# Writing the instruction order out by hand to the end of the first chunk's recurrence

## The chip, the cores and the metric

The kernel runs on one core of one Trainium2 chip. The metric is the device time of one execution in microseconds, the median of several runs. Five engines take part, each with its own queue that runs in order: PE (TensorE, matmuls), DVE (VectorE), ACT (ScalarE), POOL (GpSimd, only at the start), and SP (SyncE), which here only issues DMAs. PEld in a view is PE loading weights beside its matmuls.

## The reference

Three stages follow each other: a recurrence with gates over 768 time steps (4 batches, 8 heads of 40 channels), then two gated feed-forward layers on its 3072 x 320 output.

```python
# recurrence, per batch and head, for each t
m_new = np.maximum(f_gate[t] + m, i_gate[t])
f_stab, i_stab = np.exp(f_gate[t] + m - m_new), np.exp(i_gate[t] - m_new)
C = f_stab * C + i_stab * outer(v[t], k[t])
n = f_stab * n + i_stab * k[t]
y[t] = sigmoid(o_gate[t]) * (C @ q[t]) / np.maximum(np.abs(n @ q[t]), 1.0)
# first layer, 320 -> 1536 -> 320
x = (sigmoid(x @ w_gate) * (x @ w_val)) @ w_out
# second layer, 320 -> 2048 -> 320
h = x @ w_in
out = (h * np.clip(h + 3, 0, 6) / 6) @ w_out
```

All of it is fp32.

## The kernel before

The sequence is cut into six chunks of 128 steps. A chunk of the four batches gives 512 tokens, and these go through both layers with the tokens along the free axis. The recurrence of chunk c and batch b is three pieces: `att0` (scores q.k in `scores`, the decay factors by a scan in `decays`, values scaled by the input gate, `values_end`, `weigh`), `att1` (`outputs`, `denominators`, `gated`, `state`) and `att2` (three PE transposes, then a split of the result into a high part xh on ACT and a low part xl on DVE). The decay scan of L385 needs rows of the gate factors spread over all partitions. For chunk 0 and batches 0 and 1 PE does that (`spread`); for all others a DMA reads them back from a DRAM buffer, `fz_dram` (`dec_load`, L219), which a store on SP fills first. `later_chunks` does this store for chunks 1 to 5 (L291) after a small DVE write (L289, L290), then the scan of L292, two groups of five small transposes (L278) with copies to iT and gT, and five products (L301) for one matmul (L305).

Every fp32 matmul is done as three matmuls in a reduced format, with each operand split into a high and a low part. So every weight tile has to be converted. Its 64-bit source comes by DMA into one of three `raw` buffers (`fetch`, L88); ACT makes `u` (L98), DVE the fp32 bits (L115, L118), ACT the high part (L139, L141, or L161 for an output weight) and DVE the low part (L147, L151, or L167, L170). The conversions stand in the list `jobs`: two input weights, one output weight, and so on.

The first layer is a row of steps. A step is `m1_h` (16 matmuls, L547 to L554, into two PSUM banks), on ACT a sigmoid (L573), on DVE the product g (L574), on ACT its high part gh (L560), on DVE its low part gl (L561), and later `m1_out` (eight matmuls, L589 and L599, into three banks of the pool `acc`). In chunk 0 the first four weight tiles are used in halves: first all four on batches 0 and 1 (256 columns), then all four on batches 2 and 3. The other steps have 512 columns. In what follows blocks 1 to 4 are the four steps on the first half, and step 4 is the next one.

The pools of PSUM banks hold three `mm`, three `acc` and two `att`. A tile that finds no free bank waits until a reader of an older one is done.

Two things set the order. Inside `tc.manual_schedule()` (L656 to L719) every engine gets its instructions in the order in which the code is written. Behind it a scheduler orders them by its own costs, and it may also put instructions of later code between the written ones where the engine has nothing ready by these costs. `tc.issue_after(i)` holds instructions back until i is placed. Before the change the written order ends with the transposes of batches 0 and 1 (L709), two conversions and their state; pieces of batches 2 and 3 of chunk 0 are handed out among the first steps by the loop at L746, together with `work`, which converts one or two weight tiles a step.

Of the kernel before, what the change touches and what calls it, by code (L numbers as in the profile page):

```python
# [18 lines left out]
B, H, S, D = 4, 8, 768, 40  # L19
# [7 lines left out]
T = B * L  # L27
F1 = 1536 // P
# [4 lines left out]
def mlstm_then_two_gated_ffn(  # L33
# [69 lines left out]
    def to_f32(r, u=None):  # L103

        lower = r.bitcast(I32).rearrange("p (n two) -> p two n", two=2)[:, 0, :]
        u = scaled(r) if u is None else u
        bits = gpool.tile([P, 640], I32, tag="bits", name="bits")
        nc.vector.tensor_scalar(  # L115
            out=bits, in0=u.bitcast(I32), scalar1=3, scalar2=None, op0=ALU.logical_shift_left
        )
        nc.vector.scalar_tensor_tensor(  # L118
            out=bits, in0=lower, scalar=29, in1=bits,
            op0=ALU.logical_shift_right, op1=ALU.bitwise_or,  # L120
        )
        return bits.bitcast(F32)
# [11 lines left out]
    def hi_in(key, x):  # L134


        w = new_slot(key)
        xm = x[:, 0:512].rearrange("p (j n) -> p j n", j=2)
        nc.scalar.copy(out=w[:, :, 0:256], in_=xm)  # L139
        for j, a, b in halves_in:  # L140
            nc.scalar.copy(out=w[a, j, 256:384], in_=x[a, 512:640])  # L141
        return w

    def lo_in(w, x):
        wf = w.bitcast(F32)
        xm = x[:, 0:512].rearrange("p (j n) -> p j n", j=2)
        nc.vector.tensor_tensor(  # L147
            out=w[:, :, 384:640], in0=xm, in1=wf[:, :, 0:256], op=ALU.subtract
        )
        for j, a, b in halves_in:  # L150
            nc.vector.tensor_tensor(  # L151
                out=w[b, j, 256:384], in0=x[a, 512:640], in1=wf[a, j, 256:384], op=ALU.subtract
            )
# [4 lines left out]
    def hi_out1(key, x):  # L158

        w = new_slot(key)  # L160
        nc.scalar.copy(out=w[:, :, 0:320], in_=x.rearrange("p (j n) -> p j n", j=2))  # L161
        return w

    def lo_out1(w, x):
        wf = w.bitcast(F32)
        r = x.rearrange("p (j n) -> p j n", j=2)
        nc.vector.tensor_tensor(  # L167
            out=w[:, :, 320:384], in0=r[:, :, 256:320], in1=wf[:, :, 256:320], op=ALU.subtract
        )
        nc.vector.tensor_tensor(  # L170
            out=w[:, :, 384:640], in0=r[:, :, 0:256], in1=wf[:, :, 0:256], op=ALU.subtract
        )
# [45 lines left out]
    def dec_load(c, b):  # L218
        nc.sync.dma_start(  # L219
            out=at[c, b]["dec"].rearrange("p h l -> p (h l)"),  # L220
            in_=fz_dram[c, b * H : (b + 1) * H, :]
            .rearrange("h l -> (h l)")
            .rearrange("(o n) -> o n", o=1)
            .to_broadcast([P, H * L]),
        )
# [7 lines left out]
    def stabilise(a, b):  # L233


        m_old, m_new = m_sb[:, a:b], m_sb[:, a + 1 : b + 1]
        f, i = f_sb[:, a:b], i_sb[:, a:b]
        nc.vector.tensor_tensor_scan(
            out=m_new, data0=f, data1=i,
            initial=-1e30 if a == 0 else m_sb[:, a : a + 1], op0=ALU.add, op1=ALU.max,  # L240
        )
        yield
        nc.vector.tensor_tensor(out=f, in0=f, in1=m_old, op=ALU.add)
        yield
        nc.vector.tensor_tensor(out=f, in0=f, in1=m_new, op=ALU.subtract)
        yield
        nc.scalar.activation(out=fz_sb[:, a:b], in_=f, func=AF.Exp)
        yield
        nc.vector.tensor_tensor(out=i, in0=i, in1=m_new, op=ALU.subtract)
        yield  # L250
        last_exp.append(nc.scalar.activation(out=i, in_=i, func=AF.Exp).ins)
        yield
# [151 lines left out]
    def out_gate(c, b):  # L404
        o = at[c, b]["vko"][:, 2, :]
        nc.scalar.activation(out=o, in_=o, func=AF.Sigmoid)
# [118 lines left out]
    def att2(c, b, ps):  # L525
        yo = at.pop((c, b))["yo"]
        x_ps = ps()
        for k in range(3):
            nc.tensor.transpose(
                out=x_ps[:, k * P : (k + 1) * P], in_=yo[:, k * P : (k + 1) * P], identity=ident  # L530
            )
        x_v = x_ps[:, : 3 * P].rearrange("p (k t) -> p k t", k=3)
        xs = slice(b * L, (b + 1) * L)
        hi = nc.scalar.copy(out=XH[1, c][:, :, xs], in_=x_v)
        lo = nc.vector.tensor_tensor(
            out=XL[1, c][:, :, xs], in0=x_v, in1=XH[1, c].bitcast(F32)[:, :, xs], op=ALU.subtract
        )
        return hi.ins, lo.ins
# [87 lines left out]
    jobs = []  # L626
# [29 lines left out]
    with tc.manual_schedule():  # L656
        qk_load(0, 0)
        vko_load(0, 0)
        qk_load(0, 1)
        raws = [fetch(jobs[-1][0])]  # L660
        vko_load(0, 1)
        for _ in stabilise(0, L):
            pass
        nc.sync.dma_start(out=fz_dram[0], in_=fz[:, 0, :])
        raws += [fetch(jobs[-2][0]), fetch(jobs[-3][0])]
        for b in range(2, B):
            qk_load(0, b)
            vko_load(0, b)
            dec_load(0, b)
        later = stabilise(L, S)  # L670
        first, second = spread(0), spread(1)
        next(later)
        next(later)
        next(first)
        transpose_rows(i_c, iT, range(0, 1))
        decays(0, 0, 0)
        next(first)
        next(later)
        next(later)
        decays(0, 0, 1)  # L680
        scores(0, 0, any_ps)
        value_ones(0, 0)
        values(0, 0, False)
        u = scaled(raws[0])
        values_end(0, 0, False)
        next(later)
        next(later)
        for n in range(2):
            weigh(0, 0, n)
            next(second)  # L690
        x0 = to_f32(raws[0], u)
        scores(0, 1, any_ps)
        for n in range(2):
            decays(0, 1, n)
        value_ones(0, 1)
        values(0, 1, False)
        values_end(0, 1, False)
        for b in range(2):
            out_gate(0, b)
        w0 = hi_in(jobs.pop()[2], x0)  # L700
        outputs(0, 0, any_ps)
        for n in range(2):
            weigh(0, 1, n)
        outputs(0, 1, any_ps)
        gated(0, 0, denominators(0, 0), False)
        u = scaled(raws[1])
        lo_in(w0, x0)
        gated(0, 1, denominators(0, 1), False)
        for b in range(2):  # L709
            opened = att2(0, b, any_ps)  # L710
        x1 = to_f32(raws[1], u)
        w1_ = hi_in(jobs.pop()[2], x1)
        u = scaled(raws[2])
        lo_in(w1_, x1)
        x2_ = to_f32(raws[2], u)
        wo_ = hi_out1(jobs.pop()[2], x2_)
        lo_out1(wo_, x2_)
        for b in range(2):
            state(0, b)  # L719

    with tc.issue_after(opened[0]), tc.issue_after(opened[1]):
        later_chunks()
# [10 lines left out]
    steps = [step for c in range(NC) for step in tile_steps(c)]  # L733


    pieces = [(0, b, piece) for b in (2, 3) for piece in range(3)]
    for c in range(1, NC):
        for b in range(B):
            pieces += [(c, b, 0)] + [(c, b - 1, 2)] * (b > 0) + [(c, b, 1)]
# [2 lines left out]

    quota = [2, 2] + [1] * 4 + [0, 1] * 4 + [1] * (n_first - 14) + [1, 1, 0, 1, 0, 1]
    quota += [1] * (len(steps) - len(quota))
    before = []
    for i, (c, f, ts) in enumerate(steps):  # L746
        if i == halves[0] - 1:
            for b in range(2):
                att_load(1, b)
                dec_load(1, b)  # L750
        for _ in range(quota[i]):
            if pieces:
                cp, b, piece = pieces.pop(0)
                if cp > 0 and b == 0 and piece == 0:
                    x_tiles((1, cp))
                with ExitStack() as queued:
                    for ins in opened if cp == 0 else ():
                        queued.enter_context(tc.issue_after(ins))
                    (att0, att1, att2)[piece](cp, b, ps_att)
                nxt = divmod(cp * B + b + 2, B)  # L760
                if cp > 0 and piece == 2 and nxt[0] < NC:
                    att_load(*nxt)
                    dec_load(*nxt)
        gate = m1_h(c, f, ts)
        if before:
            m1_out(*before)
            if before[1] == F1 - 1:
                m1_end(before[0])
        before = (c, f, ts)
        if c == 0:  # L770
            work(1 if i < 2 * halves[0] else 2, n_w1)
        elif c < NC - 1:

            with tc.issue_after(gate):
                work(c > 1 and f % 2 == 0, n_conv)
        elif f == 0:
            work(F2, n_conv)
        else:
            work(f > 1, n_jobs)
        if c == NC - 1 and f == 6:  # L780
            x_split(0)
# [125 lines left out]
```

## Time and profile before

| | us |
|---|---|
| median of 3 runs | 875.86 (875.47 to 877.73) |
| the profiled execution | 874.0 |
| its span | 872.0 |
| PE busy / idle in the span | 844.7 / 27.3 |
| DVE busy | 516.2 |
| ACT busy | 347.5 |

Busy time is the sum over the whole span. The kernel has stages with different limits, so a share of 59% for DVE says nothing of a stretch of 50 us; the view by stretches does. The 27.3 us of PE idle are 872.0 less 844.7.

### The profile page before, as it was taken

How to read it: one execution, taken by the hardware profiler on the slowest of the kernel's cores; microseconds unless marked ns; L12 is line 12 of the kernel's file. 1: busy time of each engine (PE TensorE's matmuls, PEld its weight loads, DVE VectorE, ACT ScalarE, POOL GpSimd, SP SyncE). 2: the span in 40 equal slices, each digit the busy share in tenths (PEclk: the TensorE clock that was granted, in tenths of full speed). 3: DMA queues.
4: the chain of work that ended last, by engine and by line, in shares of the span. 5: the costliest groups of instructions: out<-in, count | busy, mean ns of one | idle time of the engine just before them, and what ended most of it. 6: DMA issues, size and time to landing. Idle time of an engine off the chain costs nothing.

```text
span 872.0 us, 17027 instructions
## 1 busy us (share of the span) xinstructions
PE 844.7 (97%) x7205; PEld 726.5 (83%) x7205; DVE 516.2 (59%) x930; ACT 347.5 (40%) x685; POOL 2.5 (0%) x8
## 2 busy tenths in 40 slices
PE   6599999999999999999999999999999999999998
PEld 6488678888788878878888888999999999999997
DVE  7899967776676777667545544344343353443433
ACT  3687634222333332342226445343343343433333
POOL 1000000000000000000000000000000000000000
PEclk9999999999999999999999999999999999999999
DMA  9645632232444355454203321001010010000000
GB/s 351 233 139 184 232 103 109 81 135 71 154 162 157 123 198 161 164 181 162 80 1 97 91 82 73 1 25 43 1 67 1 1 67 2 31 1 1 31 1 30
DMA packets 24923, 83.43 MB, mean 96 GB/s; under 512 B 2576, under 2 KB 5840, under 8 KB 24848
## 3 DMA queue, kind: packets, MB, share of 16 engines
q1 hardware_dynamic: 24800, 82.26, 27.7%
q8 instruction: 56, 0.92, 0.4%
q14 instruction: 19, 0.16, 0.1%
q10 hardware_dynamic: 48, 0.10, 0.0%
HBM read 68.35 MB, written 13.99 MB: 94 GB/s over the span
## 4 chain that ended last, share of the span: by engine, by line
PE 83%; DVE 4%; DMA 2%; issue 1%; ACT 0%; DVEq 0%
PE mm L551 11%; PE mm L553 11%; PE mm L552 11%; PE acc L589 10%; PE mm L547 6%; PE mm L554 6%; PE acc L813 5%; PE acc L812 5%; PE acc L811 5%; PE acc L599 3%; PE att L359 2%; DMA dec<-fz_dram 2%; PE att L813 2%; PE att L812 2%; PE att L811 2%; PE att L441 1%
## 5 line engine op out<-in xcount | busy, mean ns | idle before, releaser
L551 PE MATMUL mm<-xh,w 128*128 128x512 f32 (+1 forms) x520 | 195.8, 376 | 0.2 <-issue 0.2
L553 PE MATMUL mm<-xh,w 128*128 128x512 f32 (+1 forms) x520 | 194.8, 375 | 0.0
L552 PE MATMUL mm<-xl,w 128*128 128x512 f32 (+1 forms) x520 | 194.8, 375 | 0.0
L560 ACT CAST gh<-g 128x512 fp32r<-128x512 f32 (+1 forms) x178 | 106.1, 596 | 202.9 <-DVE g L574 111.5
L561 DVE TENSOR_TENSOR gl<-g,gh 128x512 fp32r<-128x512 f32 (+1 forms) x178 | 117.7, 661 | 112.9 <-ACT gh L560 112.3
L793 DVE SCALAR_TENSOR_TENSOR g<-g,mm 128x512 f32<-128x512 f32 x96 | 66.1, 689 | 112.0 <-ACT g L792 111.9
L553 PEld LDWEIGHTS mm<-xh,w 128*128 128x128 f32 x520 | 98.3, 189 | 18.6
L552 PEld LDWEIGHTS mm<-xl,w 128*128 128x128 f32 x520 | 98.3, 189 | 18.5
L792 ACT ACTIVATE g<-mm,half 128x512 f32<-128x512 f32 x96 | 66.2, 690 | 112.1 <-PE mm L554 112.0
L551 PEld LDWEIGHTS mm<-xh,w 128*128 128x128 f32 x520 | 98.5, 189 | 14.6 <-issue 0.4
L589 PE MATMUL acc<-gh,w 128*128 128x512 f32 (+1 forms) x328 | 104.8, 364 | 1.4 <-ACT gh L560 1.4
L547 PE MATMUL mm<-xl,w 128*128 128x512 f32 (+1 forms) x260 | 104.1, 401 | 1.1 <-ACT g L573 1.1
L554 PE MATMUL mm<-xh,w 128*128 128x512 f32 (+1 forms) x260 | 97.2, 374 | 0.0
L813 PE MATMUL acc<-w,gl 128*128 128x320 f32 x288 | 89.0, 309 | 0.0
L812 PE MATMUL acc<-w,gh 128*128 128x320 f32 x288 | 88.9, 309 | 0.0
L811 PE MATMUL acc<-w,gh 128*128 128x320 f32 x288 | 88.8, 308 | 0.0
L574 DVE TENSOR_TENSOR g<-g,mm 128x512 f32<-128x512 f32 (+1 forms) x82 | 50.7, 619 | 57.1 <-PE mm L554 56.5
L573 ACT ACTIVATE g<-mm 128x512 f32<-128x512 f32 (+1 forms) x82 | 44.8, 546 | 94.1 <-PE mm L554 93.9
L589 PEld LDWEIGHTS acc<-gh,w 128*128 128x128 f32 x328 | 60.5, 189 | 11.9 <-ACT gh L560 2.1
L589 PE MATMUL acc<-gl,w 128*128 128x512 f32 (+1 forms) x164 | 60.3, 368 | 2.1 <-DVE gl L561 2.0
L547 PEld LDWEIGHTS mm<-xl,w 128*128 128x128 f32 x260 | 49.1, 189 | 10.7 <-ACT g L573 1.5
L554 PEld LDWEIGHTS mm<-xh,w 128*128 128x128 f32 x260 | 49.1, 189 | 8.7
(154 smaller groups left out, 1074.4 us busy)
## 6 DMA issues: line engine op xcount, KB each, us to landing
raw<-in_w SPq DMA_DIRECT2D x20, 640.0 KB, 4.1
qk<-in_qkT SPq DMA_DIRECT2D x22, 512.0 KB, 5.1
vko<-in_vko SPq DMA_DIRECT2D x22, 480.0 KB, 4.1
dec<-fz_dram SPq DMA_DIRECT2D x20, 512.0 KB, 5.6
raw<-in_wo SPq DMA_DIRECT2D x14, 640.0 KB, 4.0
w_dram<-bits SPq DMA_DIRECT2D x16, 320.0 KB, 2.4
raw<-w_dram SPq DMA_DIRECT2D x16, 320.0 KB, 2.9
x_dram<-x SPq DMA_DIRECT2D x6, 768.0 KB, 4.7
```

What stands on the lines that cost most here:

```text
L547: nc.tensor.matmul(out=banks[j], lhsT=tail, rhs=xl[:, 2, :], start=True, stop=False)
L551: nc.tensor.matmul(out=banks[j], lhsT=hi, rhs=xh[:, k, :], start=False, stop=False)
L552: nc.tensor.matmul(out=banks[j], lhsT=hi, rhs=xl[:, k, :], start=False, stop=False)
L553: nc.tensor.matmul(out=banks[j], lhsT=lo, rhs=xh[:, k, :], start=False, stop=False)
L554: nc.tensor.matmul(out=banks[j], lhsT=tail, rhs=xh[:, 2, :], start=False, stop=True)
L560: nc.scalar.copy(out=gh, in_=g)
L561: nc.vector.tensor_tensor(out=gl, in0=g, in1=gh.bitcast(F32), op=ALU.subtract)
L589: nc.tensor.matmul(out=a[m], lhsT=lhsT, rhs=rhs, start=st and lhsT is hi and rhs is gh, stop=en and lhsT is lo, skip_group_check=True,)
L792: nc.scalar.activation(out=g[j], in_=banks[j], func=AF.Relu, scale=1.0 / 6.0, bias=half)
L811: nc.tensor.matmul(out=a, lhsT=gh[:, ts], rhs=hi, start=st, stop=False)
L812: nc.tensor.matmul(out=a, lhsT=gh[:, ts], rhs=lo, start=False, stop=False)
L813: nc.tensor.matmul(out=a, lhsT=gl[:, ts], rhs=hi, start=False, stop=en)
```

## The change

The written order goes on. In place of two conversions it now holds the rest of chunk 0's recurrence (batches 2 and 3), blocks 1 to 4 with the first layer's output matmuls of blocks 1 to 3, and five conversions (with the one before them six). All six raw tiles are fetched in the written part. `later_chunks` is held back behind the split of batch 2 (it was behind that of batch 1). The loop over steps starts at step 4.

```diff
+        raws += [fetch(jobs[-1 - n][0]) for n in range(3, 6)]
         later = stabilise(L, S)
...
         for b in range(2):
-            opened = att2(0, b, any_ps)
-        x1 = to_f32(raws[1], u)
...
+            att2(0, b, any_ps)
+        ts = slice(0, T // 2)
+        x = to_f32(raws[1], u)
+        decays(0, 2, 0)
+        w = hi_in(jobs.pop()[2], x)
+        u = scaled(raws[2])
+        lo_in(w, x)
+        m1_h(0, 0, ts)
+        scores(0, 2, ps_att)
+        value_ones(0, 2)
+        x = to_f32(raws[2], u)
+        w = hi_out1(jobs.pop()[2], x)
+        lo_out1(w, x)
+        m1_h(0, 1, ts)
+        m1_out(0, 0, ts)
         for b in range(2):
             state(0, b)
+        for b in range(2, B):
+            out_gate(0, b)
+        u = scaled(raws[3])
+        decays(0, 2, 1)
+        values(0, 2, False)
+        values_end(0, 2, True)
+        for n in range(2):
+            weigh(0, 2, n)
+        m1_out(0, 1, ts)
+        outputs(0, 2, ps_att)
+        x = to_f32(raws[3], u)
+        w = hi_in(jobs.pop()[2], x)
+        gated(0, 2, denominators(0, 2), False)
+        lo_in(w, x)
+        u = scaled(raws[4])
+        m1_h(0, 2, ts)
+        opened = att2(0, 2, ps_att)
+        scores(0, 3, ps_att)
...
+        x = to_f32(raws[4], u)
+        outputs(0, 3, ps_att)
+        w = hi_in(jobs.pop()[2], x)
+        gated(0, 3, denominators(0, 3), False)
+        lo_in(w, x)
+        u = scaled(raws[5])
+        m1_h(0, 3, ts)
+        att2(0, 3, ps_att)
+        x = to_f32(raws[5], u)
+        w = hi_out1(jobs.pop()[2], x)
+        lo_out1(w, x)
+        m1_out(0, 2, ts)
+        state(0, 3)
...
-    pieces = [(0, b, piece) for b in (2, 3) for piece in range(3)]
+    pieces = []
...
-    before = []
-    for i, (c, f, ts) in enumerate(steps):
-        if i == halves[0] - 1:
+    before = steps[halves[0] - 1]
+    for i, (c, f, ts) in list(enumerate(steps))[halves[0] :]:
+        if i == halves[0]:
```

Place 1 is DVE at block 1, whose product is L574 and low part L561. Before the change its row there reads:

```order
L350 TENSOR_TENSOR y<-att,den 128x8x40
L574 TENSOR_TENSOR g<-g,mm 128x256
L499 TENSOR_TENSOR yo<-y,early 128x320
L151 TENSOR_TENSOR w<-bits,w 64x128 x2
L561 TENSOR_TENSOR gl<-g,gh 128x256
L118 SCALAR_TENSOR_TENSOR bits<-raw,bits 128x640
```

In the changed kernel DVE has these rows around the same two:

```order
L147 TENSOR_TENSOR w<-bits,w 128x2x256
L151 TENSOR_TENSOR w<-bits,w 64x128 x2
L574 TENSOR_TENSOR g<-g,mm 128x256
L561 TENSOR_TENSOR gl<-g,gh 128x256
L115 TENSOR_SCALAR bits<-u 128x640
L118 SCALAR_TENSOR_TENSOR bits<-raw,bits 128x640
```

Two kinds of other work stood between the product and the low part; now the two follow each other, here and in blocks 2 to 4.

Place 2 is DVE from the small write L290, after which SP may store the gate factors of the later chunks, to the product of block 4. Before, the write stands early, among the scans of batches 2 and 3:

```order
L289 COPY early<-early 32x5
L385 SCALAR_TENSOR_TENSOR early<-early,ident_78 128x512
L118 SCALAR_TENSOR_TENSOR bits<-raw,bits 128x640
L290 MEMSET early 32x5
L385 SCALAR_TENSOR_TENSOR early<-early,ident_78 128x512
L350 TENSOR_TENSOR vi<-early,iT 128x8x40
L147 TENSOR_TENSOR w<-bits,w 128x2x256
```

and now it comes a dozen instructions ahead of the scans of chunk 1 (`dec<-dec`), which have moved in front of block 4's product:

```order
L290 MEMSET early 32x5
L400 TENSOR_TENSOR early<-att,early 128x4x128 x2
L115 TENSOR_SCALAR bits<-u 128x640
...
L147 TENSOR_TENSOR w<-bits,w 128x2x256
L151 TENSOR_TENSOR w<-bits,w 64x128 x2
L385 SCALAR_TENSOR_TENSOR dec<-dec,ident_78 128x512 x4
L574 TENSOR_TENSOR g<-g,mm 128x256
L561 TENSOR_TENSOR gl<-g,gh 128x256
L535 TENSOR_TENSOR xl<-att,xh 128x3x128
```

Before, one scan of chunk 1 stood behind block 2 and the other behind block 4; now all four of batches 0 and 1 stand in one place.

Place 3 is SP's queue at the store of the gate factors (L291) and the two loads of chunk 1 that read them (L219, `dec`). Before:

```order
L291 DMA fz_dram<-early 32x5x128
L88 DMA raw<-in_w 128x640
L88 DMA raw<-in_wo 128x640
L219 DMA dec<-fz_dram 128x1024
L211 DMA vko<-in_vko 128x960
L219 DMA dec<-fz_dram 128x1024
```

After:

```order
L211 DMA vko<-in_vko 128x960
L88 DMA raw<-in_wo 128x640
L88 DMA raw<-in_w 128x640
L291 DMA fz_dram<-early 32x5x128
L219 DMA dec<-fz_dram 128x1024 x2
```

Raw fetches that stood behind the store now stand ahead of it, and the two loads follow the store at once.

## Rows read from the trace of the kernel before

**Rows 1.** The page: busy time by engine, and PE and DVE in forty slices.

```profile
PE 844.7 (97%) x7205; PEld 726.5 (83%) x7205; DVE 516.2 (59%) x930; ACT 347.5 (40%) x685; POOL 2.5 (0%) x8
...
PE   6599999999999999999999999999999999999998
...
DVE  7899967776676777667545544344343353443433
```

**Rows 2.** Windows: start:end, length, busy us (instructions) per engine, clock, DMA.

```profile
30.00:40.00 10.00, 2.64 (x65) 2.10 (x67) 9.91 (x20) 7.46 (x22) 0.00 (x0) 1.00 0.61 189
40.00:60.00 20.00, 20.00 (x285) 18.38 (x277) 18.38 (x44) 17.31 (x57) 0.00 (x0) 1.00 0.54 183
50.00:60.00 10.00, 10.00 (x172) 9.19 (x172) 9.60 (x24) 8.34 (x27) 0.00 (x0) 1.00 0.43 136
60.00:110.00 50.00, 45.14 (x493) 37.15 (x492) 49.04 (x102) 32.79 (x83) 0.00 (x0) 1.00 0.59 201
70.00:80.00 10.00, 8.29 (x59) 7.31 (x60) 9.89 (x20) 7.14 (x21) 0.00 (x0) 1.00 0.58 195
```

**Rows 3.** Timeline of PE: start, length, what, and idle time before it.

```profile
35.69 0.36 PE L452 MATMUL att<-vi,early 128*32 128x41 f32 x8 [5.60 <-DVE early L400]
37.08 0.74 PE L278 MATMUL mm<-ident,early 32*128 32x32 f32 x5 [1.02 <-DVE early L292]
38.56 0.71 PE L305 MATMUL mm<-ge,par 32*128 32x80 f32 x2 [0.74 <-DVE ge L301]
...
40.87 0.58 PE L547 MATMUL mm<-xl,w 128*128 128x256 f32 x1
...
41.46 0.41 PE L552 MATMUL mm<-xl,w 128*128 128x256 f32 x1
41.68 0.41 PE L553 MATMUL mm<-xh,w 128*128 128x256 f32 x1
...
59.02 0.39 PE L547 MATMUL mm<-xl,w 128*128 128x256 f32 x1
...
60.92 0.28 PE L554 MATMUL mm<-xh,w 128*128 128x256 f32 x1
...
63.25 0.78 PE L441 MATMUL att<-cst,qk 128*32 128x82 f32 x32 [1.09 <-DVE dec L400]
...
65.21 0.28 PE L552 MATMUL mm<-xl,w 128*128 128x256 f32 x1
```

**Rows 4.** Timeline of DVE, from the last split of batch 1 on.

```profile
27.03 0.56 DVE L535 TENSOR_TENSOR xl<-att,xh 128x384 fp32r<-128x384 f32 x1 [0.75 <-ACT xh L534]
...
62.41 1.28 DVE L400 TENSOR_TENSOR dec<-att,dec 128x512 f32<-128x512 f32 x2
```

**Rows 5.** Groups of ACT by line, 27.5 to 64 us: busy, mean ns | idle before.

```profile
L560 ACT CAST gh<-g 128x256 fp32r<-128x256 f32 x4 | 1.6, 392 | 0.0
L161 ACT CAST w<-bits 128x640 fp32r<-128x640 f32 x2 | 1.4, 720 | 0.8 <-DVE bits L118 0.8
```

**Rows 6.** The same of DVE: the scans of chunk 1.

```profile
L385 DVE TENSOR_TENSOR_SCAN dec<-dec,ident 128x512 f32<-128x512 f32 x2 | 2.4, 1222 | 0.0
```

**Rows 7.** SP's DMA issues: start, length, what.

```profile
29.95 0.34 SPq L291 DMA_DIRECT2D fz_dram<-early  x1
...
35.52 0.38 SPq L219 DMA_DIRECT2D dec<-fz_dram  x1
```

**Rows 8.** DMA issues by tile: KB of one, median us to landing.

```profile
dec<-fz_dram SPq DMA_DIRECT2D x20, 512.0 KB, 5.6
...
fz_dram<-early SPq DMA_DIRECT2D x1, 80.0 KB, 1.8
```

**Rows 9.** The answer on L219, the loads of the gate factors: their spread.

```profile
DMA to landing us min/median/max: 4.3/5.6/9.4
```

**Rows 10.** The chain that ended last: start, length, what.

```profile
106.36 0.73 DVE bits L118
...
107.75 1.42 PE acc L589 x5
```

More of the change, by code (lines that the diff above doesn't have):

```diff
@@ L709, in mlstm_then_two_gated_ffn @@
         for b in range(2):
-            opened = att2(0, b, any_ps)
-        x1 = to_f32(raws[1], u)
-        w1_ = hi_in(jobs.pop()[2], x1)
-        u = scaled(raws[2])
[L714 to L717, printed above, removed]
+            att2(0, b, any_ps)
[3 more added lines that the diff above has]
+        w = hi_in(jobs.pop()[2], x)
+        u = scaled(raws[2])
+        lo_in(w, x)
[7 more added lines that the diff above has]
+        m1_out(0, 0, ts)
         for b in range(2):
             state(0, b)
+        for b in range(2, B):
[16 more added lines that the diff above has]
+        scores(0, 3, ps_att)
+        value_ones(0, 3)
+        for n in range(2):
+            decays(0, 3, n)
+        values(0, 3, False)
+        values_end(0, 3, True)
+        for n in range(2):
+            weigh(0, 3, n)
+        state(0, 2)
+        x = to_f32(raws[4], u)
[11 more added lines that the diff above has]
+        state(0, 3)
     with tc.issue_after(opened[0]), tc.issue_after(opened[1]):
@@ L755, in mlstm_then_two_gated_ffn @@
                     x_tiles((1, cp))
[L756 to L759, printed above, removed]
+                (att0, att1, att2)[piece](cp, b, ps_att)
                 nxt = divmod(cp * B + b + 2, B)
@@ L764, in mlstm_then_two_gated_ffn @@
         gate = m1_h(c, f, ts)
[L765 to L768, printed above, removed]
+        m1_out(*before)
+        if before[1] == F1 - 1:
+            m1_end(before[0])
         before = (c, f, ts)
```

## The prediction

> **What bounds the kernel now.** I read the page first, then the windows of the first 110 us, then the timelines of PE and DVE in them. The page names PE: 844.7 us busy of a span of 872.0, and in the forty slices of 21.8 us only the first two show holes [rows 1]. So at most 27.3 us are to be had in all, and they lie early. The change touches only the stretch behind 27.5 us.
>
> The windows show what the whole-span share hides. From 30 to 110 us DVE is the busier engine: idle 0.09 us in the first ten, 1.62 in the next twenty and 0.96 in the last fifty, while PE idles 7.36 us from 30 to 40, nothing to 60, and 4.86 us from 60 to 110 [rows 2]. The chain of waits agrees: it runs through DVE until 107.75 us and through PE's matmuls from there [rows 10]. So this stretch ends when DVE has done its list. What lengthens the list's idle time lengthens the kernel, and PE's holes are mostly an effect of it.
>
> PE's holes from 30 to 40 are three: 5.60 us for the weighing of batch 2, 1.02 for the scan L292 and 0.74 for the products L301, together 7.36, and then block 1 starts at 40.87 [rows 3].
>
> **The change part by part.**
>
> *What it removes.* Block 1 needs the split of batch 1, which ends at 27.03 + 0.56 = 27.59 [rows 4], and a weight that is long converted. In the new order it stands right behind, so it starts about 13 us earlier than at 40.87. If PE alone bounded the stretch, the three holes would be filled: -7.4 us. But no DVE instruction goes away. The conversions, scans and splits are the same in number; five conversions only change place. So I take nothing for it beyond what DVE's own ledger gives, and count DVE's idle time in the new order against that of the old.
>
> *The old ledger.* From 27.5 to the end of chunk 1's first weighing at 62.41 + 1.28 = 63.7 us [rows 4], DVE idles about 0.09 + 1.62 = 1.7 us [rows 2]. The old order puts other work between a block's product and its low part, and takes conversions in where something is late.
>
> *The new ledger*, to the same point. A written order holds for every instruction behind the one that waits.
>
> - Each block's L574 is followed at once by L561, which needs the high part that ACT makes of L574's result. The cast takes 0.39 us [rows 5], and two handoffs of some 0.03 each make 0.45. Four blocks: 1.8 us. The bounds are 1.6 (the casts alone) and 3.4, if ACT is still at another 0.4 us instruction each time.
> - Block 1: PE starts at 27.6 at 0.22 us a matmul (41.46 and 41.68 in [rows 3]), so its sixteen end near 31.2. DVE has L115, L118, a scan, L147 and two L151 ahead of L574, which last about as long. 0.2 us.
> - The output weight behind block 1: L167 follows L118 at once and waits for the whole cast L161, 0.72 us [rows 5]. With handoffs 0.8 us; none only if something stood between.
> - Block 2: PE has the scores of batch 2 and this block while DVE converts; I take nothing for it.
> - Block 3: its weight's low part, L151, is DVE's last work ahead of L574, and PE cannot begin before it. So DVE waits for all sixteen matmuls. At the pace of step 4 they take from 59.02 to 60.92 + 0.28, 2.2 us [rows 3]. At the slower pace, 15 x 0.22 + 0.41 = 3.7. I take 2.2, as blocks 1 and 2 come shortly ahead of it and PE works almost without pause there.
> - Block 4: in place of the same wait, the four scans of chunk 1 stand ahead of L574, 4 x 1.2 = 4.9 us [rows 6], so the block is hidden. But the scans need loads that now start late. From L290 to the first scan DVE has twelve instructions; at 9.60/24 = 0.40 to 9.89/20 = 0.49 us each [rows 2] that is 4.8 to 5.9, I take 5.3. In the same time SP must issue the store (0.34), see it land (1.8), issue the load (0.38) and see that land (5.6) [rows 7, 8]: 8.1 us. Stall: 2.8 us. Bounds: a load of 4.3 us behind 5.9 us of work leaves 0.9, one of 9.4 us [rows 9] behind 4.8 leaves 7.1. The second load is issued some 0.4 us later and hides behind the first two scans. Before the change the store was issued at 29.95 [rows 7], and the scans waited for nothing [rows 6].
>
> Queued behind that stall on DVE are block 4's product and split, batch 3's xl, the scan L292 and the products L301. PE waits for nearly all of them in a row: the second half of chunk 1's first scores needs the bank that xl frees, the second five transposes need L292, the matmul L305 needs L301, and step 4 stands behind L305. On SP the next raw fetch stands behind both loads, but its buffer comes free only when the fifth weight has been converted, about the same time.
>
> *Sum.* 1.8 + 0.2 + 0.8 + 2.2 + 2.8 = 7.8 us of DVE idle time where it had 1.7: +6.1 us.
>
> *Check from PE.* At 63.7 the old order had done seven DVE instructions more (0.40 to 0.49 each, about 3.1 us) and two scans of 1.2 us less: 0.7 us ahead. So the new one is at that point at 63.7 - 0.7 + 6.1 = 69.1 us. Step 4 can start only about then, after L305, where it started at 59.02 [rows 3]: PE is some 10 us late. It can win back at most its 4.86 us of idle time from 60 to 110, and DVE at most its 0.96 [rows 2]. That leaves +5.2 by either count, so +6.1 stands. Behind 110 us PE is the bound with the same work.
>
> The profiled execution took 874.0 us, 2.0 more than its span; with 6.1 it would be 880.1. The median of the runs is 875.86, 1.9 above that execution, so the forecast is 875.86 + 6.1 = **882.0 us**.
>
> **A rule weighed against a row.** All these windows list the granted clock as 1.00 [rows 2], so the level shows in PE's pace alone: 256 columns each 0.22 us at 41.5 us, behind the sparse stretch, which is 1.2 GHz, and 1.9/15 = 0.13 at 59 us, which is 2.4 GHz [rows 3]. A hole of 1.09 us ahead of 63.25 changed nothing: the matmul at 65.21 lasts 0.28 us as at 60.92, where those at 41.5 lasted 0.41 [rows 3]. The Trainium skill (TensorE: Matmul & The Clock Gate, section "What's actually happening") says that the half rate is the default and that an idle stretch brings it back. The new order has holes of 2 to 3 us ahead of blocks 3 and 4 and a longer one ahead of step 4, longer than any hole that the rows show PE to pass at full rate. By that rule these blocks would run at the slow pace; by the rows around 63.25 they would not. The sum goes by the fast pace, and the slow one is rival B.
>
> **The rivals.**
>
> *A, faster: PE's early start is what counts.* PE fills the 7.36 us, and DVE's waits fall where its list has slack behind it: 875.9 - 7.4 = 868.5 us. For it: PE's 97% [rows 1] and the 5.60 us hole. It decides if DVE's new waits come to less than the 1.7 us of old, that is if the conversions that it does from 60 to 110 us are so far ahead of need that PE never sees them late. Against it: in those 50 us PE waits 4.86 us already with DVE idle for 0.96 [rows 2].
>
> *B, slower still: slow blocks and a late load.* Blocks 3, 4 and step 4 each cost 16 x 0.09 = 1.4 us more, of which block 4's is hidden by the scans: +2.9, or 884.9. With the slow load (7.1 in place of 2.8) +4.3 more: 889.2.
>
> *C, no change: the waits are real but small.* If the loads come in time (0.9) and half of block 3 is covered by a late ACT and DVE (1.1), the sum is 4.8 - 1.7 = +3.1; if the raw fetches come earlier too and PE wins back part of its idle time, some 1 to 2 us are left: 877.5.
>
> **How the numbers follow.** A measurement of this kernel tells about 0.3%, 2.6 us, from no change; its three runs lie 2.3 us apart. Forecast (slower by 3 to 9 us): 0.56. B: 0.16. C: 0.14. A: 0.14. So faster by over 0.3% 0.14, within 0.3% 0.14, slower 0.72. The range leaves out most of A and the end of B where load and pace are both slow: 873 to 889 us. The forecast's own range is 878.5 to 885.
>
> **What would show it.** Right: in the profile after, PE starts its first 256-column matmul near 27.7 us, and step 4 not at 59 but near 69; DVE has idle time of 2 us or more put down to PE ahead of block 3's L574, and 1 to 7 us put down to the DMA of `dec` ahead of the scan that precedes block 4; four waits of about 0.4 us for L560; the store of the gate factors is issued near 50 us where it was 29.95. DVE's idle time from 27.5 to 69 us is near 8 us. Wrong: the scans find their loads landed, or step 4 starts before 62 us, or PE's idle time from 60 to 110 us falls under 2 us while DVE's grows, which would be A. If blocks 3 and 4 run at 0.21 us a matmul, it is B.

## The result and the profile after

| | before | changed |
|---|---|---|
| median of four runs each, us | 876.2 (875.47 to 877.73) | 888.12 (887.34 to 888.55) |
| the profiled execution: time, span, us | 874.0, 872.0 | 887.88, 885.7 |
| PE busy, DVE busy, us | 844.7, 516.2 | 853.1, 516.9 |
| PE's idle time, us | 27.3 | 32.6 |

The changed kernel takes 1.0136 times as long (95% interval 1.0119 to 1.0153): 11.9 us slower, where 6.1 was forecast. The page after, against [rows 1]: busy time by engine, PE and DVE in forty slices, and PE's granted clock.

```profile
PE 853.1 (96%) x7205; PEld 734.3 (83%) x7205; DVE 516.9 (58%) x930; ACT 347.2 (39%) x685; POOL 2.5 (0%) x8
...
PE   6659999999999999999999999999999999999998
...
DVE  7778986776676767666644555435344343444433
...
PEclk9756999999999999999999999999999999999999
```

The work is the same in number and, on DVE, in busy time. The difference lies in slices 2 to 4, where DVE has 7, 7 and 8 in place of 8, 9 and 9, and PE's clock row 7, 5 and 6. The windows say how much; the columns are those of [rows 2]. First the kernel before, then the changed one.

```profile
27.50:80.00 52.50, 42.23 (x592) 38.45 (x593) 50.44 (x111) 37.84 (x115) 0.00 (x0) 1.00 0.53 177
```

```profile
27.50:80.00 52.50, 37.72 (x397) 33.96 (x398) 37.46 (x74) 27.04 (x86) 0.00 (x0) 0.63 0.34 117
80.00:110.00 30.00, 29.94 (x395) 26.00 (x394) 29.27 (x64) 22.76 (x57) 0.00 (x0) 1.00 0.58 203
```

DVE idles 52.50 - 37.46 = 15.04 us where it idled 2.06. That is 13.0 us more, and the span is 13.7 longer. Behind 80 us DVE is full again, and little is won back: PE starts the first step of 512 columns 14.7 us later than before (92.25 against 77.58), and the steps from 123 us on about 13 us later (123.63 against 110.65). The timeline of DVE after shows which waits make up the 15 us; the bracket at a row's end is the idle time ahead of it and what ended that.

```profile
31.17 0.42 DVE L574 TENSOR_TENSOR g<-g,mm 128x256 f32<-128x256 f32 x1 [0.33 <-ACT vko L406]
32.06 0.42 DVE L561 TENSOR_TENSOR gl<-g,gh 128x256 fp32r<-128x256 f32 x1 [0.47 <-ACT gh L560]
...
34.55 0.29 DVE L167 TENSOR_TENSOR w<-bits,w 128x128 fp32r<-128x128 f32 x1 [0.79 <-ACT w L161]
...
37.72 0.47 DVE L350 TENSOR_TENSOR vi<-early,iT 128x320 f32<-128x320 f32 x1
40.41 1.29 DVE L400 TENSOR_TENSOR early<-att,early 128x512 f32<-128x512 f32 x2 [2.23 <-ACT vd L348]
...
45.15 0.61 DVE L151 TENSOR_TENSOR w<-bits,w 64x128 fp32r<-64x128 f32 x2
49.38 0.42 DVE L574 TENSOR_TENSOR g<-g,mm 128x256 f32<-128x256 f32 x1 [3.62 <-PE mm L554]
...
53.97 0.06 DVE L290 MEMSET early<- 32x5 f32 x1
55.60 1.29 DVE L400 TENSOR_TENSOR early<-att,early 128x512 f32<-128x512 f32 x2 [1.57 <-ACT vd L348]
...
61.12 4.57 DVE L385 TENSOR_TENSOR_SCAN dec<-dec,ident 128x512 f32<-128x512 f32 x4
...
66.93 0.42 DVE L561 TENSOR_TENSOR gl<-g,gh 128x256 fp32r<-128x256 f32 x1 [0.93 <-ACT gh L560]
...
76.16 0.49 DVE L115 TENSOR_SCALAR bits<-u 128x640 int32<-128x640 int32 x1 [1.02 <-ACT u L98]
...
79.00 0.42 DVE L574 TENSOR_TENSOR g<-g,mm 128x256 f32<-128x256 f32 x1 [2.35 <-PE mm L554]
```

With two more L561 at 0.47 these come to 14.25 us. Two rows have no counterpart in the forecast: L400, which waits for `vd` of L348. `weigh` multiplies the decay factors in place, and ACT's eight L348 of `values_end` still read them. ACT's timeline after shows both groups of eight, right behind the product `vi` at 37.72 and its like at 53.37:

```profile
38.07 0.77 ACT L98 ACTIVATE u<-raw 128x640 f32<-128x640 f32 x1
38.75 1.85 ACT L348 ACTIVATE vd<-vi,early 128x41 f32<-128x41 f32 x8
...
53.92 1.87 ACT L348 ACTIVATE vd<-vi,early 128x41 f32<-128x41 f32 x8 [3.20 <-issue]
```

SP's issues after, against [rows 7]: the store leaves at 54.06 in place of 29.95, the two loads (one row) 1.76 us behind it.

```profile
54.06 0.34 SPq L291 DMA_DIRECT2D fz_dram<-early  x1
55.82 0.81 SPq L219 DMA_DIRECT2D dec<-fz_dram  x2
```

PE's timeline after, against [rows 3]: the first block, the third (first, second and last matmul) and step 4.

```profile
27.29 0.58 PE L547 MATMUL mm<-xl,w 128*128 128x256 f32 x1 [1.16 <-DVE xl L535]
...
45.49 0.58 PE L547 MATMUL mm<-xl,w 128*128 128x256 f32 x1 [2.38 <-DVE w L151]
45.87 0.41 PE L551 MATMUL mm<-xh,w 128*128 128x256 f32 x1
...
48.86 0.41 PE L554 MATMUL mm<-xh,w 128*128 128x256 f32 x1
...
60.82 0.58 PE L547 MATMUL mm<-xl,w 128*128 128x256 f32 x1 [2.15 <-DVE w L151]
...
75.11 0.58 PE L547 MATMUL mm<-xl,w 128*128 128x256 f32 x1
```

Block 1 starts at 27.29 where it started at 40.87, block 3 at 45.49 with 0.21 us a matmul, and step 4 at 75.11 where it started at 59.02.

### The profile page after: what moved, and what is told of

Its sections match the earlier page's. It is cut to its first block, busy times and chain, and to the rows that moved or that the text cites. A ratio compares the mean times of both kernels' runs of the same rounds, so it can differ in the third digit from the quotient of the medians.

```text
span 885.7 us, 17026 instructions
## 1 busy us (share of the span) xinstructions
PE 853.1 (96%) x7205; PEld 734.3 (83%) x7205; DVE 516.9 (58%) x930; ACT 347.2 (39%) x685; POOL 2.5 (0%) x8
## 4 chain that ended last, share of the span: by engine, by line
PE 84%; DVE 8%; DMA 3%; ACT 3%; issue 2%; DVEq 0%; ACTq 0%; SPq 0%
PE mm L551 11%; PE mm L553 11%; PE mm L552 11%; PE acc L589 9%; PE mm L547 6%; PE mm L554 5%; PE acc L857 5%; PE acc L856 5%; PE acc L855 5%; PE acc L599 3%; PE att L359 2%; DMA dec<-fz_dram 2%; PE att L857 2%; PE att L856 2%; PE att L855 2%
## 5 line engine op out<-in xcount | busy, mean ns | idle before, releaser
L561 DVE TENSOR_TENSOR gl<-g,gh 128x512 fp32r<-128x512 f32 (+1 forms) x178 | 117.6, 660 | 114.5 <-ACT gh L560 114.0
L553 PEld LDWEIGHTS mm<-xh,w 128*128 128x128 f32 x520 | 100.1, 192 | 18.5
L552 PEld LDWEIGHTS mm<-xl,w 128*128 128x128 f32 x520 | 100.1, 193 | 18.4
L551 PEld LDWEIGHTS mm<-xh,w 128*128 128x128 f32 x520 | 100.2, 193 | 14.9 <-issue 0.8
L574 DVE TENSOR_TENSOR g<-g,mm 128x512 f32<-128x512 f32 (+1 forms) x82 | 50.7, 618 | 62.0 <-PE mm L554 61.2
L547 PEld LDWEIGHTS mm<-xl,w 128*128 128x128 f32 x260 | 49.8, 191 | 16.3 <-DVE w L151 4.9
L554 PEld LDWEIGHTS mm<-xh,w 128*128 128x128 f32 x260 | 50.1, 193 | 8.7
```

Of the source, the lines that this page charges most:

```text
L547: nc.tensor.matmul(out=banks[j], lhsT=tail, rhs=xl[:, 2, :], start=True, stop=False)
L551: nc.tensor.matmul(out=banks[j], lhsT=hi, rhs=xh[:, k, :], start=False, stop=False)
L552: nc.tensor.matmul(out=banks[j], lhsT=hi, rhs=xl[:, k, :], start=False, stop=False)
L553: nc.tensor.matmul(out=banks[j], lhsT=lo, rhs=xh[:, k, :], start=False, stop=False)
L554: nc.tensor.matmul(out=banks[j], lhsT=tail, rhs=xh[:, 2, :], start=False, stop=True)
L561: nc.vector.tensor_tensor(out=gl, in0=g, in1=gh.bitcast(F32), op=ALU.subtract)
```

## The experiments

Theory 1: the time follows DVE's idle time (and work added to DVE) up to the last conversion. Theory 2, the rival: PE's slow pace behind its holes makes the difference. Medians of the kernel before, run beside them, are 876.19, 875.1 and 875.36 us for the three sets; the ratios are to these. Each edit is against the changed kernel, except in two cases that say so. Where an edit adds lines, the numbers in rows shift.

**The wait for `vd` taken away.** The last factors are multiplied on DVE, in two instructions of 0.5 us.

```diff
-        values_end(0, 2, True)
+        values_end(0, 2, False)
...
-        values_end(0, 3, True)
+        values_end(0, 3, False)
```

> The changed kernel (888.1 us) with values_end of batches 2 and 3 on DVE (one instruction of 0.50 us each) in place of eight ACT instructions each (1.86 us). In the changed kernel DVE waits 2.23 and 1.57 us ahead of the weighing L400 until ACT has read the last column of the decay factors. Theory 1 (the time follows DVE's idle time up to the end of the conversions): 3.8 us of waits go, 1.0 us of DVE work comes: 885.3 us. Theory 2 (the time follows PE's slow pace in blocks 3, 4 and step 4, that is the 8.4 us by which PE's busy time grew): the holes ahead of the blocks stay over 2 us, the pace stays slow, at most 1 us back: 887 us or more.

Measured: 883.78 us (883.24 to 885.53), ratio 1.0091 (1.0076 to 1.0106); 4.3 less than the changed kernel. DVE's timeline shows the product standing directly ahead of the weighing, with no wait:

```profile
39.18 0.50 DVE L350 TENSOR_TENSOR vd<-vi,early 128x328 f32<-128x328 f32 x1
39.71 1.29 DVE L400 TENSOR_TENSOR early<-att,early 128x512 f32<-128x512 f32 x2
...
62.02 0.42 DVE L574 TENSOR_TENSOR g<-g,mm 128x256 f32<-128x256 f32 x1 [3.62 <-PE mm L554]
```

So this wait is a cost of the change, though not all of the 3.8 us comes back where it stood: the loop's scans moved behind block 4, whose product (the last row) then waited 3.62 us for PE. The edit thus moves work as well as taking the wait away, and the 4.3 us are those of both.

**Work put into the wait ahead of block 3.** Batch 3's scans and product `vi` stand ahead of block 3's product instead of behind it.

```diff
         u = scaled(raws[4])
+        for n in range(2):
+            decays(0, 3, n)
+        values(0, 3, False)
         m1_h(0, 2, ts)
...
-        for n in range(2):
-            decays(0, 3, n)
-        values(0, 3, False)
```

> The changed kernel with batch 3's two scans L385 and the scaling of its values (2.8 us of DVE work) ahead of block 3's product in place of behind its low part; nothing else on any engine moves. DVE waits 3.62 us for block 3's matmuls there. Theory 1: the work fills the wait, 2.7 us less idle time: 885.4 us. Theory 2 (pace): block 3 is as slow as before, and PE's hole ahead of the outputs of batch 3 gets shorter by 2.7 us of 3.9, which may keep block 4 fast (1.4 us): 886.7 us or more.

Measured: 884.58 us (883.73 to 885.86), ratio 1.0098 (1.0082 to 1.0113); 3.5 less. Nothing else moves in the order. DVE's idle time falls to 11.93, and the wait ahead of block 3 to 0.87, though PE runs that block at the same 0.21 us a matmul:

```profile
49.37 0.42 DVE L574 TENSOR_TENSOR g<-g,mm 128x256 f32<-128x256 f32 x1 [0.87 <-PE mm L554]
```

**The same work inside and outside a wait.** Two spare scans (1.2 us each, the result unused) are added in two places: in the first kernel ahead of block 3's product, in the second ahead of the outputs of batch 2, some instructions earlier, where DVE has no wait. All else is in the same order.

```diff
+        for _ in range(2):
+            nc.vector.tensor_tensor_scan(
+                out=spare, data0=ident4.rearrange("p h l -> p (h l)"),
+                data1=ident4.rearrange("p h l -> p (h l)"),
+                initial=0.0, op0=ALU.mult, op1=ALU.add,
+            )
```

> The changed kernel with two more scans on DVE (2.3 us, result read by nobody) between block 3's last weight part L151 and its product L574, where DVE waits 3.62 us for PE. The order on all engines is otherwise that of the changed kernel. Theory 1 (only DVE's idle time counts): the work falls into the wait, no change, 888.1 us and a wait of 1.3 us left. Rival (the time follows DVE's work or the length of the written order as such): +2.3, 890.4 us.

> The changed kernel with the same two scans nine DVE instructions earlier, ahead of batch 2's denominators, where DVE does not wait; otherwise the same order on all engines. Theory 1: everything behind comes 2.3 us later and no wait takes it up: 890.4 us. Theory 2 (the time follows PE's work and pace): DVE's added work is hidden in holes of 2.4 us ahead of block 3, which PE has anyway: 888 to 889 us.

Measured: 887.87 us (886.07 to 889.84), ratio 1.0140 (1.0121 to 1.0160), and 890.91 (888.53 to 891.33), ratio 1.0173 (1.0153 to 1.0193). The product of block 3 in the first and in the second:

```profile
49.69 0.42 DVE L575 TENSOR_TENSOR g<-g,mm 128x256 f32<-128x256 f32 x1 [1.07 <-PE mm L555]
```

```profile
36.76 0.42 DVE L575 TENSOR_TENSOR g<-g,mm 128x256 f32<-128x256 f32 x1 [1.45 <-PE mm L555]
...
53.17 0.42 DVE L575 TENSOR_TENSOR g<-g,mm 128x256 f32<-128x256 f32 x1 [3.62 <-PE mm L555]
```

In the wait, 2.4 us of work cost nothing and the wait shrinks by 2.55; outside it, the wait stays and the median is 3.0 us higher. Not all of the 3.0 is the edit. The first of the two rows above is block 2's product, ahead of the spare scans: it waits 1.45 us for PE, whose block 2 took 0.21 us a matmul in this execution and 0.12 in the other, with the same order up to there. Of the 3.5 us by which block 3's product comes later, 2.5 are the scans and 1.0 was there before them. The single runs of the two kernels also overlap (886.07 to 889.84 and 888.53 to 891.33). What the traces do show is that the added work vanishes in the wait and passes on in full outside it. This is theory 1 at its most direct: DVE's list, work and waits together, sets this stretch.

**PE kept busy.** Spare matmuls into an unused bank fill PE's holes ahead of blocks 3 and 4 and step 4: 16, 16, 8, 28, 14 and 24 of them at six places.

```diff
+    def warm(n):
+        ps = ps_mm()
+        for _ in range(n):
+            nc.tensor.matmul(
+                out=ps[:, 0:256], lhsT=slots["in", 0][:, 0, 0:P], rhs=XH[1, 0][:, 0, 0:256],
...
         u = scaled(raws[4])
+        warm(16)
         m1_h(0, 2, ts)
```

> The changed kernel with 106 more matmuls of 256 columns into a bank that nobody reads, in six bursts of 8 to 28 where PE has its holes behind block 2, so that PE does not stand idle ahead of blocks 3 and 4. If PE's pace is 0.12 us a matmul in blocks 3 and 4 and step 4, theory 2 (pace) expects the 8.4 us of added PE busy time back: 880 us. Theory 1 (DVE's idle time) expects only what DVE waits less: 3.62 to 2.2 us ahead of block 3's product and 2.35 to about 0.5 ahead of step 4's, so 3 us: 885 us. If the pace does not rise, nothing is gained and the bursts may cost up to 1 us.

Measured: 887.81 us (887.42 to 888.77), ratio 1.0135 (1.0120 to 1.0150): no difference. PE's timeline at block 3 (the spare matmuls, then the first two and the last), and the last matmul of step 4:

```profile
43.31 2.18 PE L572 MATMUL mm<-xh,w 128*128 128x256 f32 x16
45.82 0.36 PE L547 MATMUL mm<-xl,w 128*128 128x256 f32 x1 [0.34 <-DVE w L151]
46.02 0.28 PE L551 MATMUL mm<-xh,w 128*128 128x256 f32 x1
...
47.69 0.28 PE L554 MATMUL mm<-xh,w 128*128 128x256 f32 x1
...
76.32 0.41 PE L554 MATMUL mm<-xh,w 128*128 128x256 f32 x1
```

The block runs at 0.12 us a matmul in place of 0.21, as does block 4; step 4 stays at 0.21, so the edit takes the slow pace from the blocks alone. DVE's wait ahead of its product falls from 3.62 to 2.09 us. But in the window from 27.5 to 80 us

```profile
27.50:80.00 52.50, 46.81 (x597) 42.69 (x600) 38.42 (x77) 27.06 (x85) 0.00 (x0) 0.87 0.35 117
```

DVE still idles 14.08 us: part of what the wait lost comes back as a new one of 1.99 us for ACT's `vi` of chunk 1. Theory 2 expected 8 us with all three at the fast pace; with two of them nothing came back, and theory 1's 885 us was missed by 2.8. That the pace is not the main cause shows fully only in the last kernel of the set below in which the waits are filled: there step 4 runs at 0.12 us too, and the time is no better. The pace sets the length of single waits.

**The store early, and two scans late.** These go by the prediction's reason, the late loads. In the first kernel `later_chunks` is held back behind batch 1's split, as before the change, so the store leaves at 29.46. In the second, two of chunk 1's scans stand behind block 4.

```diff
-            att2(0, b, any_ps)
+            opened = att2(0, b, any_ps)
...
-        opened = att2(0, 2, ps_att)
+        att2(0, 2, ps_att)
```

```diff
-        att2(0, 3, ps_att)
+        held = att2(0, 3, ps_att)
...
+                    for ins in held if (cp, b, piece) == (1, 0, 0) else ():
+                        queued.enter_context(tc.issue_after(ins))
```

> The changed kernel with later_chunks held back behind the split of batch 1 as before the change: the store of the gate factors goes out near 29 us in place of 54, the loads come early, and chunk 1's four scans move from ahead of block 4's product to the weighing of batch 2. The theory of the prediction (late loads and the scans in front of block 4 cost 2.8 us and more): 884 us. Theory 1 (DVE's idle time alone counts): one scan fills 1.1 us of the wait for ACT ahead of batch 2's weighing, but behind block 4's weight DVE must now wait some 3.3 us for the sixteen slow matmuls that the scans hid: 888 to 890 us.

> The changed kernel with the first piece of chunk 1 held back behind the split of batch 3: two of the four scans ahead of block 4's product go behind that split; the store stays late. The theory of the prediction: block 4's product, the split, the scores of chunk 1 and with them step 4 come 2.3 us earlier: 886 us. Theory 1: DVE waits about 1.1 us for block 4's matmuls in place of scanning, nothing else goes: 888 to 889 us.

Measured: 888.40 (887.86 to 889.59), ratio 1.0155 (1.0139 to 1.0172), and 887.97 (887.02 to 888.91), ratio 1.0149 (1.0132 to 1.0166): neither gains. SP's issues in the first, and then its DVE timeline at the first of chunk 1's scans and at block 4's product:

```profile
29.46 0.34 SPq L291 DMA_DIRECT2D fz_dram<-early  x1
34.44 0.38 SPq L219 DMA_DIRECT2D dec<-fz_dram  x1
```

```profile
40.26 1.22 DVE L385 TENSOR_TENSOR_SCAN dec<-dec,ident 128x512 f32<-128x512 f32 x1 [0.85 <-DMA dec<-fz_dram]
...
68.88 0.42 DVE L574 TENSOR_TENSOR g<-g,mm 128x256 f32<-128x256 f32 x1 [3.63 <-PE mm L554]
```

The scans are done by 47.6 us, but then they no longer cover block 4, whose product waits 3.63 us, and the time is the same. The place of the scans is not what was lost.

**The waits filled together.** `vd` on DVE; one scan of batch 3 ahead of block 3's product; and between each block's product and its low part a scan or the first step of a conversion (in block 3 batch 3's other scan and `vi`).

```diff
-        gs[c, f, ts.start] = split_g(g)
+        gs[c, f, ts.start] = split_g(g, between)
...
         nc.scalar.copy(out=gh, in_=g)
+        if between:
+            between()
...
-        m1_h(0, 2, ts)
+        decays(0, 3, 0)
+        m1_h(0, 2, ts, lambda: (decays(0, 3, 1), values(0, 3, False)))
```

The second kernel has the early store too, the third the spare matmuls.

> The changed kernel with three edits that take DVE's waits away and no work: values_end of batches 2 and 3 on DVE, batch 3's scans around block 3's product, and in blocks 1 to 4 a scan or a conversion's first half between the product L574 and the low part L561. Theory 1 (DVE's idle time): the first two alone gave 4.3 and 3.5 us, four waits of 0.47 to 0.93 for the cast are 2.3 more: 888.1 - 10.1 = 878 us, at most 880.5 if they overlap. Theory 2 (PE's pace): PE's holes ahead of blocks 3 and 4 stay, so 883 us.

> The three fills of e5 and the early store of e6 together. Theory 1: the waits that chunk 1's scans fill are gone already, so what e6 gives or costs comes on top of e5 with little of its gain: 877 to 880 us, in no case below the kernel before (876.2). Theory 2: 882 us or more.

> The three fills of e5 (882.0 us) with bursts of matmuls of which nobody reads the result, as in e2, and one burst of 14 more ahead of step 4. In e5 DVE still waits 2.06 us for block 3 and 3.96 for step 4, both at the slow pace. Theory 1: at the fast pace these waits shrink by 1.4 and 1.9 us: 879 us, and still above the kernel before, since DVE's idle time stays over its 2.1. Theory 2 (pace is what is left): 874 us or less.

Measured: 881.97 (881.32 to 883.51), ratio 1.0082 (1.0067 to 1.0097), 882.61 (881.99 to 884.88), ratio 1.0091 (1.0076 to 1.0106), and 889.78 (888.20 to 891.85), ratio 1.0167 (1.0146 to 1.0188). The first is the best of all variants, 6.1 us under the changed kernel, and still 6.9 over the kernel before: no L561 waits in it, but 2.06 us for PE at block 3, 1.16 for the scores at L400 and 3.96 for step 4 are left. It missed theory 1's 878 to 880.5 us and lies nearer to theory 2's 883. The second missed theory 1's range by 2.6 us, for the reason just shown (block 4's product waits 3.63), and by its time alone it fits theory 2's 882 or more. So these two don't tell the theories apart. The third fits neither theory: theory 1 had 879 us, theory 2 at most 874. PE's clock stands at 0.97 in it up to 80 us, where the changed kernel has 0.63, and DVE idles 7.98 us:

```profile
27.50:80.00 52.50, 46.27 (x644) 43.41 (x644) 44.52 (x94) 27.09 (x78) 0.00 (x0) 0.97 0.43 150
```

So the fast pace alone wins nothing. At the step that starts at 112 us it is 9.1 us behind the kernel before (the first variant 7.6), since DVE waited for PE behind spare matmuls, and by the next step it has lost 5.2 us more. So its smaller idle time up to 80 us didn't shorten it, against theory 1. PE's timeline there:

```profile
114.80 0.50 PE L547 MATMUL mm<-xl,w 128*128 128x512 f32 x1 [0.82 <-ACT g L584]
119.12 0.49 PE L600 MATMUL acc<-gh,w 128*128 128x512 f32 x1 [2.19 <-ACT gh L560]
120.60 0.79 PE L600 MATMUL acc<-gl,w 128*128 128x512 f32 x1 [0.98 <-DVE gl L563]
```

There the loop's order, which the scheduler makes and which followed the edit, is another one. Why it put these so is open.

**More and less work on DVE in the kernel before.** Both edits are against the kernel before: three spare scans behind the last split of batch 1, and products of `vi` and `yo` given to POOL.

```diff
+        for _ in range(3):
+            nc.vector.tensor_tensor_scan(out=spare, ...)
```

```diff
-        nc.vector.tensor_tensor(
+        (nc.gpsimd if (c == 1 or (c == 0 and b > 1)) else nc.vector).tensor_tensor(
```

> The kernel before (876.2 us) with three more scans of the kind of L385 at the end of its written order, whose result nobody reads: 3 x 1.14 = 3.4 us more DVE work ahead of the first block. Theory 1 (up to some 108 us the kernel ends when DVE has done its list): all of it is seen, 879.6 us. Theory 2 (PE bounds this stretch too, DVE's work is hidden): not over 877.5 us.

> The kernel before (875 to 876 us) with less DVE work in the stretch that DVE bounds: the gating product L499 of batches 2 and 3 of chunk 0 and of chunk 1 (6 x 0.49 us) and the scaling of the values of batches 2 and 3 (2 x 0.46) go to POOL, which is idle there. Theory 1 (the kernel before ends this stretch when DVE has done its list): up to 3.9 us less, 872.5 us or a little more, as POOL's results come later. Rival (PE bounds the kernel before there, or the two engines get in each other's way): 875 us or more.

Measured: 884.28 (881.70 to 886.82), ratio 1.0083 (1.0062 to 1.0104), and 877.40 (875.95 to 879.01), ratio 1.0023 (1.0012 to 1.0033). Neither settles anything, though by its time alone the second fits the rival's 875 us or more and not theory 1's 872.5. In the first the scheduler reordered all that follows, and three scans of 1.2 us cost 8.1. In the second PE is 1.2 us early at block 1 and 3.3 late at the step that starts at 113.94 us; between them it waits 1.54 us for POOL, whose products last about twice DVE's 0.49. The groups of POOL:

```profile
L504 POOL TENSOR_TENSOR yo<-y,vko 128x320 f32<-128x320 f32 x4 | 3.5, 870 | 92.0 <-ACT y L348 50.9 <-DVE y L350 41.1
L504 POOL TENSOR_TENSOR yo<-y,early 128x320 f32<-128x320 f32 x2 | 2.1, 1058 | 28.7 <-ACT w L139 17.8 <-DVE y L350 10.9
```

**All together.** DVE's idle time from 27.5 to 80 us (with work added to DVE counted in: 1.0 for `vd`, 2.4 for spare scans), less the 2.06 of before; then what the span of that same execution has over the 872.0 of before; then the median's excess over the kernel before:

| kernel | idle and added | span | median |
|---|---|---|---|
| waits filled | 9.2 | 8.2 | 6.9 |
| scans ahead of block 3 | 9.9 | 9.8 | 8.4 |
| filled, store early | 11.3 | 10.8 | 7.5 |
| `vd` on DVE | 12.0 | 11.7 | 7.6 |
| PE kept busy | 12.0 | 14.0 | 11.6 |
| work in the wait | 12.9 | 16.0 | 12.5 |
| changed kernel | 13.0 | 13.7 | 11.9 |
| two scans late | 14.0 | 13.3 | 12.9 |
| work outside the wait | 14.1 | 16.6 | 15.6 |
| store early | 15.2 | 14.1 | 13.3 |
| filled, PE kept busy | 6.9 | 14.4 | 14.4 |

But for four kernels the span follows the idle time within 1.1 us. By the medians the three that move `vd` would come out 2.3 to 4.4 us better than their idle time, but that sets the idle time of one execution against the median of others: the profiled one of `vd` on DVE is the slowest of its four (885.53 us), and its span, 11.7, agrees with its 12.0. Of the four, the work outside the wait has step 4's wait of 2.34 us behind 80 us, where the count ends; with PE kept busy and with the work in the wait, PE starts the step of 110.65 us before by 12.3 and 13.3 us late, near their 12.0 and 12.9, and loses the rest behind it; the last one is the open case above.

## Why the prediction was right or wrong

**Right: what bounds, and the sign.** That DVE's list sets the stretch [rows 2], that no work goes away and that the waits count in full held: the spare scans and batch 3's work put into the wait show it. Block 1 did start at once (27.29 against 27.6), and PE's 7.36 us of holes brought nothing, so rival A and rival C fell. The nothing that was taken for block 2 was luck: in two other executions (`vd` on DVE and the work outside the wait), with the same order up to there, PE ran that block at 0.21 us a matmul and its product waited 1.25 and 1.45 us.

**Wrong: the new ledger.** Its terms against the trace after, us:

| term | forecast | measured |
|---|---|---|
| four L561 | 1.8 | 2.34 |
| block 1 | 0.2 | 0.33 |
| L167 | 0.8 | 0.79 |
| block 2 | 0 | 0 |
| block 3 | 2.2 | 3.62 |
| block 4: stall for `dec` | 2.8 | 0 |
| L400 for ACT's `vd` | not in it | 3.80 |
| behind the ledger's end: L115, step 4 | not in it | 3.37 |

*The step that failed is the list of waits itself.* I followed what each DVE instruction reads from ACT (L561, L167), but not what it overwrites. L400 writes into the factors that ACT's L348 reads; the old order put other work between the two, the new one puts them side by side, twice. Moving `vd` to DVE took both waits away and 4.3 us off the time.

*The stall for `dec` was mis-sized because of it.* I counted 5.3 us of DVE work from L290 to the first scan against 8.1 of DMA. With the 1.57 us wait for `vd` in between it took 61.12 - 53.97 = 7.15 us, and the loads, issued at 55.82, landed within 5.3 us. That the scans find their loads landed was one of the prediction's signs of being wrong. One unseen wait hid another that I had counted: in the first kernel with the waits filled, where the wait for `vd` is gone, a scan does wait for its load, though only 0.82 us.

```profile
57.14 3.46 DVE L385 TENSOR_TENSOR_SCAN dec<-dec,ident 128x512 f32<-128x512 f32 x3 [0.82 <-DMA dec<-fz_dram]
```

Where that store was issued early, nothing was won.

*The ledger ended too early.* I stopped it at the first weighing of chunk 1 and let PE's lateness count no further. But step 4, late at 75.11 (forecast near 69), makes DVE wait 2.35 us for it, and the conversion ahead of it 1.02 for ACT. The check from PE allowed both engines to win back at most 4.86 and 0.96 us; DVE won nothing.

**The rule that was weighed.** Blocks 3 and 4 and step 4 ran at 0.21 us a matmul, 1.2 GHz. The holes of 2.38 and 2.15 us right ahead of the blocks did not bring that about: PE's granted clock had fallen before them. The windows of the changed kernel, ahead of block 3, in the hole and in the block:

```profile
38.80:42.20 3.40, 0.73 (x54) 0.63 (x57) 1.75 (x4) 2.16 (x10) 0.00 (x0) 1.00 0.00 0
42.40:45.40 3.00, 0.71 (x43) 0.55 (x32) 2.83 (x8) 1.96 (x5) 0.00 (x0) 0.50 0.37 128
45.40:49.00 3.60, 3.51 (x16) 3.51 (x17) 0.33 (x2) 0.46 (x2) 0.00 (x0) 0.50 0.20 82
```

Before it fell, PE had been idle for 2.40 us and had then done short matmuls of 41 columns. Ahead of block 4 it stands at 0.50 from 52.8 us on, and stays there through step 4. With spare matmuls in these holes block 3 ran at 0.12 us, 2.4 GHz. So far the trace agrees with the Trainium skill (TensorE: Matmul & The Clock Gate, section "What's actually happening"), that an idle stretch brings the half rate back. Here rival B had the pace right: block 3 cost 1.4 us more than the forecast's 2.2. But the slow load that made B's upper figure didn't occur, so it is luck that the time lies near that figure; and the fast pace by itself was worth nothing in the median, as the spare matmuls showed.

**Left open.** Why the filled kernel with spare matmuls, with the least idle time up to 80 us, is none the faster and loses 5.2 us between 112 and 125 us; and whether DVE work taken out of the kernel before would shorten it in full, which POOL's slower products kept from showing. Nor did any edit give back more than 6.1 of the 11.9 us (5.0 if each kernel is set against the kernel before that ran beside it); for the rest the cause is read from the trace's waits alone. No variant beat the kernel before; its DVE idles 2.06 us in this stretch, so by theory 1 a written order had at most about that to win.

## What to carry to other kernels

Where one engine has hardly any idle time, as DVE here with 2.06 of 52.5 us, a new order of the same work has little to win and every new wait to lose. List for each instruction of that engine not only whose result it reads but who still reads what it overwrites, with in-place updates first. Carry the list on until the order is the old one again, since a producer that is made late makes its consumer wait once more. An unfilled wait is worth something only to work that has to be done anyway: moving two scans and a product of 2.8 us into one gained 3.5 us.

## What the runs showed of the hardware

The granted clock in the record and PE's pace do not always go together. Before, 256 columns took 0.22 us at 41.5 us while the record shows 1.00 [rows 2, 3]. In the kernel with work outside the wait block 2 ran at 0.21 us, and the record has 1.00 there too (32.6 to 35.0 us). In the changed kernel they agree: block 3 at 0.21 us stands in a window at 0.50, shown above. A window must be short for that, since one from 40 to 60 us mixes the two levels to 0.64. The pace of equal matmuls in the timeline is the safer reading. And POOL took 0.87 to 1.06 us on average for a product of 128 by 320 for which DVE took 0.49.
